# Reciprocals in four replicas, modulation rows next to the denominators, and another order of the down projection's pairs

## The chip, the cores and the metric

One core of one Trainium2 chip. The metric is the device time of one execution in microseconds (us). The program is written engine by engine: TensorE (PE in the profile; PEld are its weight loads), VectorE (DVE), ScalarE (ACT), GpSimd (POOL), and SyncE (SP), which issues nearly all DMAs.

## The reference, cut to what matters

A transformer block on x of 2048 rows by 1024 columns in bf16, with six modulation rows made from one vector c.

```python
mod = (silu(c) @ w_mod).reshape(1, 6, 1, -1)          # sa, ca, ga, sb, cb, gb
h = layernorm(x) * (1 + ca) + sa
x = x + ga * A(h)                                     # linear attention, 32 heads of 32
h = layernorm(x) * (1 + cb) + sb
x = x + gb * ((gelu(h @ w_gate) * (h @ w_up)) @ w_down)   # F = 3584

def A(h):
    q, k, v = heads(h @ wqkv)
    pq, pk = phi(q), phi(k)       # where(t > 0, t + 1, exp(t)) + 1e-6
    kv = einsum('bhsd,bhse->bhde', pk, v)
    z = einsum('bhsd->bhd', pk)
    num = einsum('bhqd,bhde->bhqe', pq, kv)
    den = einsum('bhqd,bhd->bhq', pq, z)[..., None] + 1e-6
    return merge(num / den) @ wo
```

## The kernel before, in words

Rows of x come in 16 chunks of 128, four to a group. The order of work on TensorE is the order in which the program calls its helpers; each helper hands operations to a scheduler object that finds the waits from the bytes that they touch. From the first k tiles to the end of the second FFN unit the orders of VectorE, ACT and GpSimd are rearranged by a small planner (`reorder`, with a table of costs); TensorE's and SP's orders stay as written, and in the down projection all orders are as written.

**Attention.** After keys and queries, 24 tiles `m_tile(g, k)` (L895) multiply phi(k) with the normalised rows, eight groups g of four heads, three column parts k; ACT copies each tile out (L900). When a group is whole, a DMA transpose (`m_t`, L703, tile mtb) turns it, and `kv_prod(g)` (L913) forms its kv blocks, which VectorE masks into KVT (L920). `w2_pair(i)` (L1201) multiplies kv blocks with wo rows into W2, 64x64 tiles of the array at a time; ACT or VectorE copies W2 out (L1208). `wo_mm` (L1283) then multiplies phi(q) with W2 and VectorE adds the result to x (L1291).

What happens between the tiles is listed in the table `HOOK` (L1302): tile number to a string of steps. `modp` and `gbr` are modulation rows: `mod_rows` (L840) sums partial products over partitions with eight matmuls onto 32 columns of the array each, ACT copies the row, and `mod_store` sends it to DRAM; two tiny loads (sbT, cbT, L1230) bring shift and scale back as columns. `den0` and `den1` are the denominators of half of the rows each: 32 matmuls onto 32 columns of the array (L1240), VectorE adds 1e-6 and takes the reciprocal (L1246) into RDC, 128 partitions (two groups, two halves, four heads of a group, eight groups g) by 256 rows, and `store` sends RDC to DRAM, scr_rd (L1248). `rb_load(sg, hs)` (L1260) brings the reciprocals back, each spread over the 32 partitions of its head: for each of the four heads of a group one DMA onto 32 partitions, 8 KB for each. `pq_scale` (L1273) multiplies phi(q) with them.

SP issues its DMAs in program order, and each waits until the DMA eight places before it has landed (eight lanes). All use one hardware queue.

**FFN.** 28 units (14 column pairs of w_gate and w_up, for each half of the rows). Each matrix product is done as one level of a 2x2 block scheme with seven products in place of eight (`prod`, numbers 1 to 7): products 1 and 2 take bf16 blocks as they are, 5, 6, 7, 3, 4 take sums of blocks in fp32r, made by VectorE (L1413, L1433). `wt_dma(u)` (L1371) loads a unit's weights. Results go to DRAM (scr_y).

**Down projection.** Eight pairs of chunks (`d_pair`), the same scheme: `d_prod(ca, b0, k)` (L1672) is 14 matmuls of 128x512 (weights are the activations' tile) of product k, operands `ya` (bf16, `y_in`, L1571), sums `sb` of ya blocks (`d_s`, L1648 on VectorE, L1643 on ACT) and sums `dt`, `dh` of w_down blocks (`d_t`, L1621), made once. A pair uses four of the eight PSUM banks, in turn with the next pair; `d_cp`, `d_ecp` (ACT) and `d_add` (VectorE) combine the products, and `evac` (L1576, L1577, then the output DMA L1578) multiplies with gb, adds x (`x_in`, L1568) and stores. `hook` calls of `hooks(i)` put DMAs and leftovers of pair 0 behind given products. Pair 0 has an order of its own (`d_pair0`), since its operands are only being made, and pair 1 still evacuates two parts of pair 0 and makes the last w_down sums.

The order of products in pairs 1 to 7, and the end of the list of steps:

```python
for k in (1, 5, 6, 2, 7, 3, 4):
...
elif k == 7:
    d_add(b0 + 3, b0 + 2)
    d_s(ca, 4)
    y_next(1)
    evac(*parts[3])
...
elif k == 3:
    evac(*parts[1])
    d_s(ca + 2, 0)
```

## Time and profile before

| What | Value |
|---|---|
| timed runs | 782.22, 783.16, 784.1 us (median 783.16) |
| profiled execution: first to last instruction | 780.9 us (780.946); it has no time of its own beside the span, and the median lies 2.2 us above it |
| granted TensorE clock | 1.000 |
| TensorE busy | 770.2 us, 99% of the span |
| VectorE busy | 645.9 us, 83% |
| ACT, GpSimd busy | 374.6 us (48%), 47.5 us (6%) |
| DMA | 130.22 MB, mean 167 GB/s; rb<-scr_rd 32 DMAs of 256 KB, 6.0 us from issue to landing |
| the tiles m, den, rows, W2 | 127.2 to 190.8 us |
| FFN units | 241.2 to 602 us (the last unit runs into the down projection) |
| down projection, pairs 1 to 7 | 623.5 to 777 us, 22.04 us for a pair |

A line of the order of time gives start, duration, engine, line, operation, output<-inputs, the shape and the count of instructions that were merged, and in brackets the idle time of the engine just before and what ended it. Weight loads are recorded at their own start, so the distance from one group's first load to the next group's is the time that the group holds TensorE.

### The profile page before, as it was taken

The page shows a single profiled execution, that of the slowest core. Times are in us where ns is not written, and L with a number is a line of the kernel's source. Part 1 is how long each engine was busy: PE and PEld are TensorE (multiplying, and loading weights), DVE is VectorE, ACT ScalarE, POOL GpSimd, SP SyncE. Part 2 cuts the span into 40 slices and gives each one's busy share as a digit, 9 for nine tenths or more (in the row PEclk, how much of TensorE's full clock was granted, in tenths as well). Part 3 has the DMA queues.
Part 4 walks back from the last instruction along what each step waited for, and adds up shares of the span by engine and source line. Part 5 has one row for each costly group of instructions (what it writes and reads, how often), then busy time and mean ns, then how long its engine had stood idle before and what let it go on. Part 6 is the DMA issues. An engine that isn't in the chain of part 4 may idle for free.

```text
span 780.9 us, 10753 instructions
## 1 busy us (share of the span) xinstructions
PE 770.2 (99%) x3825; PEld 496.2 (64%) x3883; DVE 645.9 (83%) x964; ACT 374.6 (48%) x629; POOL 47.5 (6%) x126
## 2 busy tenths in 40 slices
PE   8999999999999999999999999999999999999998
PEld 4444445666445667667676767667676576677766
DVE  6699988897899878787989888888989888676767
ACT  2497743242466487878755555555555211111111
POOL 2031300000321011100000000000000000000000
PEclk9999999999999999999999999999999999999999
DMA  9879749939999358867353865535356334443331
GB/s 284 256 167 252 158 91 215 255 80 196 203 287 231 82 138 212 230 175 215 99 145 108 250 211 172 148 96 161 97 147 221 111 127 139 144 141 114 126 125 60
DMA packets 196940, 130.22 MB, mean 167 GB/s; under 512 B 69516, under 2 KB 182420, under 8 KB 195864
## 3 DMA queue, kind: packets, MB, share of 16 engines
q1 hardware_dynamic: 196872, 129.55, 62.4%
q8 instruction: 30, 0.49, 0.3%
q14 instruction: 22, 0.18, 0.1%
q10 hardware_dynamic: 16, 0.00, 0.0%
HBM read 92.55 MB, written 23.35 MB: 148 GB/s over the span
## 4 chain that ended last, share of the span: by engine, by line
PE 95%; SPq 2%; DMA 1%; DVE 1%; issue 1%; ACT 0%; DVEq 0%; ACTq 0%
PE ps_all L1458 45%; PE ps_all L1672 21%; PE ps_all L895 7%; PE ps_all L934 7%; PE ps_all L1283 7%; PE ps_all L880 5%; PE ps_all L1593 1%; SPq L598 1%; DMA wmq<-in_w_mod_dram 1%; SPq L603 1%; DMA h1T<-xh 0%; PE ps_all L913 0%; PE ps_all L1201 0%; PE ps_all L1240 0%; DVE h1T L724 0%
## 5 line engine op out<-in xcount | busy, mean ns | idle before, releaser
L1458 PE MATMUL ps_all<-ss,tp 128*128 128x512 f32 x896 | 214.3, 396 | 0.0
L1458 PEld LDWEIGHTS ps_all<-ss,tp 128*128 128x128 f32 x896 | 168.3, 188 | 37.8 <-DVE ss L1413 0.2
L1672 PE MATMUL ps_all<-dt,sb 128*128 128x512 f32 x424 | 102.5, 398 | 0.0
L1481 ACT ACTIVATE ge<-ps_all 128x512 f32<-128x512 f32 x112 | 64.1, 597 | 73.8 <-DVE ps_all L1469 62.1
L1458 PE MATMUL ps_all<-h2a,wt 128*128 128x512 bf16 x421 | 95.7, 379 | 1.8
L1672 PEld LDWEIGHTS ps_all<-dt,sb 128*128 128x128 f32 x424 | 79.6, 188 | 18.5 <-DVE sb L1648 0.3
L1476 DVE TENSOR_TENSOR ps_all<-ps_all,es 128x512 f32<-128x512 f32 x54 | 37.6, 699 | 49.4 <-ACT es L1466 49.0
L1488 DVE TENSOR_TENSOR ys<-ge,ps_all 128x512 bf16<-128x512 f32 x112 | 74.4, 684 | 3.8 <-PE ps_all L1672 0.5
L1458 PEld LDWEIGHTS ps_all<-h2a,wt 128*128 128x128 bf16 x448 | 38.0, 98 | 57.3 <-ACT ps_all L1463 16.9
L1433 DVE TENSOR_TENSOR tp<-wt 128x1024 fp32r<-128x1024 bf16 x56 | 68.1, 1217 | 1.8 <-DMA wt<-in_B_w_up_dram 1.8
L1433 DVE TENSOR_TENSOR tp<-wt,tp 128x1024 fp32r<-128x1024 bf16 x56 | 68.2, 1218 | 0.0
L934 PE MATMUL ps_all<-h1T,wq 128*128 128x512 bf16 x256 | 56.7, 379 | 0.0
L880 PE MATMUL ps_all<-wk,h1T 128*128 128x512 bf16 x239 | 55.3, 379 | 1.1 <-DMA wk<-in_A_wqkv_dram 0.5
L1283 PE MATMUL ps_all<-w,pq 128*128 128x512 bf16 x249 | 55.7, 379 | 0.5 <-issue 0.2
L1458 PE MATMUL ps_all<-ar,tp 128*128 128x512 f32 x224 | 55.5, 390 | 0.0
L869 ACT ACTIVATE eb<-ps_all 128x512 f32<-128x512 f32 x64 | 36.3, 594 | 37.6 <-PE ps_all L880 16.0
L1672 PE MATMUL ps_all<-wd,ya 128*128 128x512 bf16 x199 | 47.5, 380 | 0.7
L1458 PEld LDWEIGHTS ps_all<-ar,tp 128*128 128x128 f32 x224 | 42.1, 188 | 8.9
L1463 ACT ACTIVATE ps_all<-ps_all 128x512 f32<-128x512 f32 x56 | 32.6, 582 | 26.8 <-PE ps_all L1458 26.5
L934 PEld LDWEIGHTS ps_all<-h1T,wq 128*128 128x128 bf16 x256 | 25.0, 98 | 30.0
L1283 PEld LDWEIGHTS ps_all<-w,pq 128*128 128x128 bf16 x256 | 24.6, 98 | 30.3 <-issue 1.1
L1643 ACT ACTIVATE sb<-ya 128x896 fp32r<-128x896 bf16 (+1 forms) x16 | 14.5, 913 | 58.8 <-PE ps_all L1672 58.8
(141 smaller groups left out, 976.3 us busy)
## 6 DMA issues: line engine op xcount, KB each, us to landing
wt<-in_B_w_gate_dram SPq DMA_DIRECT2D x28, 512.0 KB, 4.0
wt<-in_B_w_up_dram SPq DMA_DIRECT2D x28, 512.0 KB, 5.2
scr_y<-ys SPq DMA_DIRECT2D x28, 512.0 KB, 3.2
ya<-scr_y SPq DMA_DIRECT2D x14, 896.0 KB, 4.9
rb<-scr_rd SPq DMA_DIRECT2D x32, 256.0 KB, 6.0
wd<-in_B_w_down_dram SPq DMA_DIRECT2D x7, 1024.0 KB, 7.6
wmst<-in_w_mod_dram SPq DMA_DIRECT2D x6, 1024.0 KB, 6.2
wmq<-in_w_mod_dram SPq DMA_DIRECT2D x8, 512.0 KB, 7.5
```

What stands on the lines that cost most here:

```text
L869: sch.op(A, lambda e: e.activation(EB[i][:, :], PS(bank), ACTF.Exp), prd=pr(bank), wr=rng, note=f"{note}.exp")
L880: o = sch.op(T, lambda e, dc=dc: e.matmul(PS(bank), H1[sg][:, ci, dc, :], W_[:, dc, jg * 512:(jg + 1) * 512], start=(dc == 0), stop=(dc == ...
L895: o = sch.op(T, lambda e, c_=c_: e.matmul(PS(bank, 0, n), PK[c_][:, g * P:(g + 1) * P], xrow(c_, o_, o_ + n), start=(c_ == 0), stop=(c_ == ...
L934: o = sch.op(T, lambda e, dc=dc: e.matmul(PS(b), WQ[:, dc, qc * P:(qc + 1) * P], H1[sg][:, :, dc, :], start=(dc == 0), stop=(dc == NDC - 1 ...
L1283: last[half] = sch.op(T, lambda e, g=g, half=half: e.matmul(PS(b0 + half), PQ[sg][:, g, ci * P:(ci + 1) * P], W2[:, g, half * 512:(half + ...
L1433: sch.op(V, lambda e: e.tensor_tensor(TP[k][:], in0, in1 if k in (0, 2) else in1[:], ALU.subtract), rd=r0 + r1, wr=r_tp(k), deps=[x1_ops[7 ...
L1458: o = sch.op(T, lambda e, l_=l_, r_=r_, dc=dc: e.matmul(PS(b), l_, r_, start=fresh and dc == 0, stop=dc == ND2 - 1, skip_group_check=True) ...
L1463: sch.op(A, lambda e: e.activation(PS(BB + t), PS(BA + t), ACTF.Copy), prd=pr(BA + t), pwr=pr(BB + t), note="pcp")
L1476: sch.op(V, lambda e: e.tensor_tensor(PS(BC + t), PS(BC + t), ES[t][:, :], ALU.add), prd=pr(BC + t), rd=r_2k(OFF_ES[t], f"es{t}"), pwr=pr( ...
L1481: sch.op(A, lambda e: e.activation(GE[i][:, :], PS(b), ACTF.Gelu_apprx_tanh), prd=pr(b), wr=r_2k(OFF_GE[i], f"ge{i}"), note="gelu")
L1488: sch.op(V, lambda e: e.tensor_tensor(YS[s_][:, 2 * h:2 * h + 2, t, :], q(GE[i][:, :]), q(PS(b + 1)), ALU.mult), rd=r_2k(OFF_GE[i], f"ge{i ...
L1672: o = sch.op(T, lambda e, l_=l_, r_=r_, j=j, dst=dst: e.matmul(dst, l_[:, 0, :], r_, start=(k in (1, 5) or own is not None) and j == js[0] ...
```

## The change

1. The reciprocals are stored in four replicas (scr_rd has a dimension of four more; four DMAs from RDC, each to one replica), and `rb_load` brings them back with DMAs that span 128 partitions, two of the eight groups g at a time, 2 KB for each partition, with eight partitions reading one replica's row. `pq_scale` now waits for the part that it reads rather than for all loads of its half; two added dependencies keep VectorE's order (the first scale behind the second reciprocal, another behind the copy of W2 block 7).
2. The store of a denominator is a step of its own (`st0`, `st1`), behind the next transpose in SP's order.
3. `modp` goes from tile 15 to tile 16, directly ahead of `den0`, in bank 2 instead of 5; den0 uses bank 3; the second W2 pair (`w1`) directly follows den0. `gbr` directly follows `den1`, in bank 6. The loads of sbT and cbT become a step `sbl` at tile 22.
4. The first FFN unit's weights (`wt_dma(0)`) are issued right behind the reciprocals' loads instead of two chunks of wo later.
5. Pairs 1 to 6 of the down projection run products 5, 6, 7, 2, then product 1 of the next pair (`d_open`), 3, 4; product 1 of pair 1 comes ahead of the loop; pair 7 runs 5, 6, 2, 7, 3, 4. In pairs 1 to 6 product 7 starts a bank of its own (b0 + 3) and is joined by one more ACT copy and two adds (`d_join`) instead of one add. DMAs of x and the leftovers of pair 0 are moved to fit.

```diff
-    scr_rd = nc.dram_tensor("scr_rd", [NSG, 2, HPG, NG, SGW // 2], f32).ap()
+    NRP = 4
+    scr_rd = nc.dram_tensor("scr_rd", [NSG, 2, HPG, NRP, NG, SGW // 2], f32).ap()
...
         def mod_pass():
             assert mdone[0] >= 48 and not late
-            mod_rows(((2, 4, 5, hl_src),))
-            o_r = mod_store(4, 5, MROW[1], r_2k(OFF_ROW + 2048, "mrow1"), 1)
+            mod_rows(((2, 4, 2, hl_src),))
+            o_sc[0] = mod_store(4, 2, MROW[1], r_2k(OFF_ROW + 2048, "mrow1"), 1)
+
+        def mod_load():
             for dst, nt, a0 in ((SBT, "sbT", 0), (CBT, "cbT", 2)):
...
             def store():
-                o_rd[pr_] = sch.dma(Q, lambda e: e.dma_start(scr_rd[2 * pr_:2 * pr_ + 2].rearrange("s f k g t -> (s f k g) t"), RDC[:, :]),
-                          rd=r_sm("rdc"), note=f"rden{pr_}.st")
+                o_rd[pr_] = [sch.dma(Q, lambda e, r=r: e.dma_start(scr_rd[2 * pr_:2 * pr_ + 2, :, :, r, :, :].rearrange("s f k g t -> (s f k) g t"), RDC[:, :]),
+                                     rd=r_sm("rdc"), note=f"rden{pr_}.st") for r in range(NRP)]
...
         def rb_load(sg, hs=(0, 1)):
             i = sg % 2
             for h in hs:
-                for k in range(HPG):
-                    made.append(sch.dma(Q, lambda e, h=h, k=k: e.dma_start(
-                        RB[i][32 * k:32 * (k + 1), h, :, :].rearrange("p a b -> p (a b)"),
-                        scr_rd[sg, h, k:k + 1, :, :].rearrange("k g t -> k (g t)").to_broadcast([32, NG * HW])),
...
+                for g0 in range(0, NG, 2):
+                    src = scr_rd[sg, h, :, :, g0:g0 + 2, :].rearrange("k r g t -> (k r) (g t)").unsqueeze(1).to_broadcast([HPG * NRP, P // (HPG * NRP), 2 * HW])
+                    sch.dma(Q, lambda e, h=h, g0=g0, src=src: e.dma_start(
+                        RB[i][:, h, g0:g0 + 2, :].rearrange("p a b -> p (a b)"), src),
+                        wr=r_rb(i, h, g0, g0 + 2), deps=o_rd[sg // 2], note=f"rb{sg}.{h}.{g0}")
...
-        HOOK = {0: "ga", 6: "kv0", 10: "kv1", 11: "w0", 13: "kv2", 15: "modp kv3 z32", 16: "den0", 17: "w1 rb0.0 rb0.1", 18: "",
-                19: "kv4", 20: "den1 ps0.0", 21: "gbr", 22: "ps0.1", 23: "rb2.0"}
+        HOOK = {0: "ga", 6: "kv0", 10: "kv1", 11: "w0", 13: "kv2", 15: "kv3 z32", 16: "modp den0 w1", 17: "st0 rb0.0 rb0.1", 18: "",
+                19: "kv4", 20: "den1 gbr ps0.0", 22: "st1 sbl ps0.1", 23: "rb2.0"}
...
         rb_load(1)
         rb_load(2, (1,))
+        wt_dma(0)
...
-            b = b0 + {1: 0, 2: 0, 5: 3, 6: 2, 7: 2, 4: 2, 3: 1}[k] if own is None else own
+            b = b0 + {1: 0, 2: 0, 5: 3, 6: 2, 7: 3 if 0 < ca < 4 * CPG - 2 else 2, 4: 2, 3: 1}[k] if own is None else own
...
+        def d_join(b0):
+            d_ecp(b0 + 3)
+            d_add(b0 + 3, b0 + 1)
+            d_add(b0 + 2, b0 + 2)
+
+        def d_open(i):
+            b = i % 2 * 4
+            d_prod(2 * i, b, 1)
+            d_cp(b + 2, b, "dpcp")
...
-            for k in (1, 5, 6, 2, 7, 3, 4):
+            for k in ((5, 6, 2, 7, 3, 4) if last else (5, 6, 7, 2, 1, 3, 4)):
...
+                if k == 1:
+                    d_open(i + 1)
+                    hook(k)
+                    continue
                 d_prod(ca, b0, k)
-                if k == 1:
-                    d_cp(b0 + 2, b0, "dpcp")
...
+                elif k == 7:
+                    if last:
+                        d_add(b0 + 3, b0 + 2)
+                    else:
+                        d_join(b0)
+                    d_s(ca, 4)
+                    evac(*parts[3])
                 elif k == 2:
+                    y_next(1)
                     evac(*parts[0])
-                elif k == 7:
-                    d_add(b0 + 3, b0 + 2)
-                    d_s(ca, 4)
-                    y_next(1)
-                    evac(*parts[3])
...
-                4: lambda: (cb1(), wt_dma(0)),
+                4: lambda: cb1(),
...
-                    if k == 1:
-                        d_t(2, 5)
-                        d_t(2, 6)
-                    if k in (6, 2, 7):
-                        d_t(4, {6: 4, 2: 5, 7: 6}[k])
-                    if k in (6, 7):
+                    if k in (6, 2):
                         n = 1 if k == 6 else 2
                         evac(*parts_of(0)[n])
                         x_in(1, n)
+                    if k in (6, 7, 2):
+                        d_t(4, {6: 4, 7: 5, 2: 6}[k])
                 else:
-                    if k == 1:
-                        x_in(i, 0, 3, 1)
-                    elif k == 5:
-                        x_in(i, 2)
+                    if k == 5:
+                        x_in(i, 1, 2)
...
+                if more and k in (1, 4):
+                    x_in(i + 1, 3 if k == 1 else 0)
...
         d_pair0(hook0)
+        d_open(1)
+        d_t(2, 5)
+        d_t(2, 6)
```

## The prediction

> **What bounds the kernel now.** I read the page's busy times and its chain of waits first, then the order of time of TensorE's weight loads in the two places that are edited, then VectorE's and SyncE's order of time beside them.
>
> ```profile
> PE 770.2 (99%) x3825; PEld 496.2 (64%) x3883; DVE 645.9 (83%) x964; ACT 374.6 (48%) x629; POOL 47.5 (6%) x126
> ...
> PE 95%; SPq 2%; DMA 1%; DVE 1%; issue 1%; ACT 0%; DVEq 0%; ACTq 0%
> ```
>
> TensorE carries 95% of the chain that ends last. So only two things can move the end: TensorE's own stream getting shorter, or a new wait in it. Both edited stretches, 165 to 200 us and 598 to 777 us, already run without one wait for data (the listing of waits gives matmuls no releaser there), so no earlier load can pay by itself. What is left in TensorE's stream shows as idle time ahead of weight loads.
>
> ```profile
> 165.55 1.26 PEld L895 LDWEIGHTS ps_all<-xall,pk 128*128 128x128 bf16 x9
> 167.09 0.12 PEld L840 LDWEIGHTS ps_all<-hl,ones 128*32 128x32 bf16 x8 [0.28 <-issue]
> 167.63 0.45 PEld L913 LDWEIGHTS ps_all<-mtb,wv 128*128 128x128 bf16 x8 [0.42 <-issue]
> ...
> 183.88 1.26 PEld L895 LDWEIGHTS ps_all<-xall,pk 128*128 128x128 bf16 x9
> 185.42 0.12 PEld L840 LDWEIGHTS ps_all<-hlg,ones 128*32 128x32 bf16 x8 [0.28 <-issue]
> 185.75 0.84 PEld L895 LDWEIGHTS ps_all<-xrow,pk 128*128 128x128 bf16 x7 [0.21 <-issue]
> 186.64 1.26 PEld L895 LDWEIGHTS ps_all<-xall,pk 128*128 128x128 bf16 x9
> ```
>
> Nine loads of a plain tile that is followed by another take 1.30 us from their start to the next load; ahead of a stretch of narrow tiles they take 1.54 (183.88 to 185.42).
>
> ```profile
> 645.54 2.71 PEld L1672 LDWEIGHTS ps_all<-wd,ya 128*128 128x128 bf16 x14 [0.26 <-issue]
> 648.36 6.35 PEld L1672 LDWEIGHTS ps_all<-dt,sb 128*128 128x128 f32 x28
> 654.98 2.70 PEld L1672 LDWEIGHTS ps_all<-wd,ya 128*128 128x128 bf16 x14 [0.26 <-issue]
> 657.80 6.35 PEld L1672 LDWEIGHTS ps_all<-dt,sb 128*128 128x128 f32 x28
> 664.18 3.13 PEld L1672 LDWEIGHTS ps_all<-dh,sb 128*128 128x128 f32 x14
> 667.58 2.71 PEld L1672 LDWEIGHTS ps_all<-wd,ya 128*128 128x128 bf16 x14 [0.26 <-issue]
> ```
>
> This is one pair of the down projection, 22.04 us, and the next one repeats it to the hundredth.
>
> **The change part by part.**
>
> *Rows beside the denominators.* Three stretches of narrow tiles lose their own place among the 128-wide tiles: the eight matmuls of the modulation rows go directly ahead of den0, the first units of W2 (pair 1) directly behind den0, the gb rows directly behind den1. What a stretch costs beyond its columns: with the gb rows, 183.88 to 186.64 is 2.76 us; without them 1.30 + 1.02 = 2.32; so 0.44 for two rounds of 256 columns, which take 0.108 each inside den's own stretch: 0.22. The modulation rows: 1.54 + 0.54 + 0.41 - 1.30 - 0.54 = 0.65, less two rounds of 512 columns at 0.216: 0.22. The W2 units (172.38 to 175.37): 2.99 - 2.32 = 0.67, less 2 x 0.23: 0.21. The rows have den's tile shape (128x32), so I take their 0.22 twice, less two hundredths each: 0.20 + 0.20. The W2 units are 64x64; the trace has no step from 128x32 to 64x64. Bounds: 0.21 saved, if the step is free, or nothing, if it costs as much as leaving for 128-wide tiles and coming back; I take the middle, 0.10. Sum 0.50, between 0.40 and 0.61.
> By the Trainium skill, TensorEngine Tiling (Array Packing), Key Properties, a change of the tiling mode, though not of the tile, drains TensorE. The idle loads above bear that out; by it the W2 stretch keeps one of its two drains, and the sum would be 0.50 as well, where a count by stretches alone gives 0.61.
>
> *Down pairs in another order.* Before, a pair runs bf16, 28 fp32r, bf16, 28 + 14 fp32r; afterwards (pairs 1 to 6) 5, 6, 7, 2, then product 1 of the next pair, 3, 4: one bf16 stretch in place of two. From the lines above, 14 fp32r matmuls in the middle of a run take 3.17 us (the stretch of 42 from 657.80, 9.78, less the one of 28 from 648.36, 6.61 before rounding); so 28 of them are 6.35 and the stretch shows 6.61: 0.26 for entering and leaving. A bf16 stretch of 14 is 2.82 where 14 x 0.216 is 3.02: 0.20 back. A switch pair costs 0.06 to 0.07 net. Fourteen changes into fp32r become eight: 6 x 0.065 = 0.39 saved. The matmuls are the same in number and kind.
>
> *What it adds.* Each pair 1 to 6 gains an ACT copy (L1698, 0.60) and a VectorE add (L1695, 0.70), since product 7 has a bank of its own. ACT has 7 to 8 us free per pair; VectorE is busy 14.9 of 22.04 us in a pair from the third on, so there both hide. But product 5 now follows product 4 directly, and its first operand (L1648, the sums of the next pair) is made after product 3: product 3's last load, 0.42 to VectorE's start (686.23 to 686.65 in the trace), two evacuation steps 1.41, half a sum 1.09 = 2.92 of the 3.17 that product 4 lasts. Margin 0.25, so nothing in the steady pairs. In pair 1 VectorE has more to do:
>
> ```profile
> 640.82 0.69 DVE L1695 TENSOR_TENSOR ps_all<-ps_all,de 128x512 f32<-128x512 f32 x1
> 641.54 0.70 DVE L1576 TENSOR_TENSOR ps_all<-ps_all,gbb 128x512 f32<-128x512 f32 x1
> ...
> 645.49 0.69 DVE L1576 TENSOR_TENSOR ps_all<-ps_all,gbb 128x512 f32<-128x512 f32 x1
> 646.28 0.69 DVE L1577 TENSOR_TENSOR xq<-ps_all,xq 128x512 bf16<-128x512 f32 x1
> 647.06 2.09 DVE L1648 TENSOR_TENSOR sb<-ya,ya 128x896 fp32r<-128x896 bf16 x2
> ```
>
> It runs without a gap from 633.8 to 652.5, with four leftovers of pair 0 and three weight sums (L1621, 1.21 each). The first half of the sums ends at 647.06 + 1.09 = 648.15, and TensorE takes it at 648.36: 0.21 to spare. The new add is one more step of 0.62 to 0.79 ahead of it on the same engine, while product 5 is due at the same moment as before, since product 1 only moved ahead of 3 and 4. So the half ends at 648.8 to 648.9, and TensorE waits 0.45 to 0.7, once: I take 0.55. Behind the late sums stand the sums for product 6 (due 3.17 later, made 2.1 later) and the evacuation of part 2; both catch up.
>
> *The reciprocals.* Instead of one store (128 KB) and eight loads onto 32 partitions each, there are four stores and eight loads onto 128. SP issues six DMAs more, and now sends: row store, transpose mT4 (waits for ACT's copy of tile 17, about 175.1), four stores, eight loads, mT5, gb row store, mT6, four stores, sbT, cbT, mT7, then as before. Who waits: kv5 for mT5, kv6 and kv7 for mT6 and mT7.
>
> ```profile
> 176.69 3.76 SPq L1260 DMA_DIRECT2D rb<-scr_rd  x8
> 180.55 1.23 SPq L703 DMA_TRANSPOSE mtb<-mb  x1
> ```
>
> Transfers land in the order of issue. Before: first load lands at 180.26, the eighth at 188.62 (1.16 to 1.2 apart), mT5 at 189.58, kv5 begins at 190.28. Afterwards: mT4 issued by 176.4, four stores at 0.35 to 0.81 to about 178, the last landing 2.24 after its issue, 180.2; first load 3.2 later, 183.4. A 2,048-byte packet onto 128 partitions takes 84 to 89 ns, an 8,192-byte packet of the old loads 605, so a load needs 8 x 0.087 = 0.70 instead of 1.16: the eighth lands at 188.3, mT5 0.96 later, 189.3, and kv5 comes at 190.28 - 0.48 = 189.80. Hidden, with 0.5 to spare; with 1.16 it would be 192.5. mT7 is issued at 190.5 (when ACT has copied tile 23), lands 3.07 later if nothing is in its way, 193.6, up to 194.6 behind sbT and cbT (3.9 each from issue); kv7 comes at 194.5. I take 0.1 for both places. sbT and cbT, moved by 17 us, are first read at 213.1 (L1767).
>
> *The first unit's weights*, moved ahead of the h2 transposes, and the second reciprocals only gain: VectorE's 1.45 us wait at 199.83 and its 1.8 us wait for wt at 224.04 should go. No matmul waits for either, so they are worth nothing at the end. The transposes come no later: SP has issued the two loads by about 204, and ACT ends the first transpose's rows at 209.8.
>
> **Sum.** -0.50 - 0.39 + 0.55 + 0.1 = -0.24 us on the profiled span of 780.95: 780.7. The timed median 783.16 lies 2.2 above that span, so 782.9.
>
> **Rivals.** (B) No new wait at all: -0.50 - 0.39, 782.2 (782.0 with the larger tile saving). For it: every margin above is positive except the one in pair 1; against it: that one is short by a whole add. (C) Slower: mT5 is late. If the loads keep 1.16, mT5 lands at 192.5 and kv5 waits 2.7, mT7 another 0.5 to 1: -0.89 + 0.55 + 3.4 = +3.1, 786.2; it decides from 0.77 per load on, and half-way (stores landing 1 us later) the time is 783.9 to 784.5. For it: the loads start 3.7 later than before; against it: the packets of other loads. By the Trainium skill, SBUF — State Buffer, The DMA setup-cost knee, every transfer pays about 2 us whatever its size; four stores paid one after another would be an estimated 8 us and kv5 over 4 us late, 787; the trace speaks against it, since old loads issued 0.45 apart land 1.16 apart. (D) Slower: the margin of 0.25 fails in all later pairs, 5 x 0.3 to 0.6 = 1.5 to 3: 784.4 to 786. For it: VectorE has a step more and the operand half the slack; against: 14.9 of 22 us busy.
>
> **How the numbers follow.** Forecast 0.48 (782.3 to 783.7), B 0.22, C 0.14, D 0.10, another gain 0.06. A difference of 0.2% is 1.57 us, about what a measurement of this kernel can tell from no change; the three runs shown spread by 1.9. Faster by more needs twice the savings found: 0.07 with a part of B's tail. Slower by more: most of C and D, 0.22. The rest, 0.71, within. Range: from below B, 781.8, to the middle of C and D, 785.2.
>
> **What would show it.** In the changed profile: no narrow stretch at 167 or 185, den's stretches 0.5 us longer; TensorE pairs of 21.97 us; one wait for VectorE (L1648's sums) of about half a microsecond at pair 2's product 5; loads 0.7 apart; mT5 landed before kv5. Wrong if kv5 or kv7 names a DMA, or if the wait at product 5 comes back in each pair.

## The result

The changed kernel takes 786.85 us (median of 5, 786.26 to 787.23) where the kernel before takes 782.59 on the same chip: 1.0050 times, 95% interval 1.0038 to 1.0062. It is slower by 4.3 us; the forecast was 782.9. The profiled execution took 786.26, its span is 784.46 us, 3.51 more than the span before (780.95).

Where it went, from the first weight loads of the same steps in both traces:

| stretch, us | before | after | difference |
|---|---|---|---|
| start to den1's first load | 182.00 | 181.39 | -0.61 (0.29 of it is there at 160 us already, before any changed step) |
| den1 to the FFN's first load | 59.24 | 63.74 | +4.50 |
| FFN to down's first dh product | 380.21 | 380.13 | -0.09 |
| down's first dh product to the end | 159.49 | 159.20 | -0.29 |

So the parts that were meant to save TensorE time do save, and the attention's last 60 us lose more. In the page of the changed kernel, TensorE's busy time hardly differs (770.2 before). In the chain that ended last DMA has 2% instead of 1%:

```profile
PE 771.2 (98%) x3829; PEld 497.2 (63%) x3883; DVE 647.7 (83%) x970; ACT 376.7 (48%) x635; POOL 48.2 (6%) x126
...
PE 95%; SPq 2%; DMA 2%; issue 1%; DVE 1%; DVEq 0%
```

Read in the order of time, this chain has a piece that was not there before (start, duration), the transpose mT5:

```profile
185.51 7.01 DMA mtb<-mb
```

The list of TensorE's waits names it (total, number, longest):

```profile
PE ps_all L914 <- DMA mtb<-mb: 2.8, 1, 2.8
```

That is kv5, waiting for the transpose mT5. TensorE's order of time around it, after:

```profile
188.27 1.47 PE L896 MATMUL ps_all<-xall,pk 128*128 128x342 bf16 x9
192.57 0.62 PE L914 MATMUL ps_all<-mtb,wv 128*128 128x128 bf16 x8 [2.83 <-DMA mtb<-mb]
193.25 3.19 PE L1288 MATMUL ps_all<-w,pq 128*128 128x512 bf16 x7
196.36 0.74 PE L1204 MATMUL ps_all<-wo,kvt 64*64 64x512 bf16 x8
```

The nine weight loads ahead of kv5 hold TensorE for 4.44 us; elsewhere nine such loads hold it for 1.31: +3.13. But the row below is odd as well. The seven matmuls of 512 columns start 427 ns apart, twice their usual 216: the granted clock fell (columns: window, its length, busy time of PE, PEld, DVE, ACT, POOL, clock, share of the DMA engines, GB/s).

```profile
189.50:192.50 3.00, 0.24 (x2) 0.00 (x0) 2.08 (x3) 0.46 (x1) 0.00 (x0) 1.00 1.16 159
193.20:196.60 3.40, 3.35 (x11) 1.06 (x14) 0.45 (x2) 0.00 (x0) 0.00 (x0) 0.51 0.74 138
```

And this is what SP sent in that time, after (start, duration of the issuing):

```profile
174.62 1.26 SPq L704 DMA_TRANSPOSE mtb<-mb  x1
175.93 2.51 SPq L1255 DMA_DIRECT2D scr_rd<-rdc  x4
180.35 5.06 SPq L1267 DMA_DIRECT2D rb<-scr_rd  x8
185.51 1.36 SPq L704 DMA_TRANSPOSE mtb<-mb  x1
186.98 0.54 SPq L850 DMA_DIRECT2D scr_row<-mrg  x1
187.62 3.86 SPq L704 DMA_TRANSPOSE mtb<-mb  x1
191.57 2.49 SPq L1255 DMA_DIRECT2D scr_rd<-rdc  x4
194.10 0.59 SPq L1237 DMA_DIRECT2D sbT<-scr_row  x1
194.75 0.68 SPq L1237 DMA_DIRECT2D cbT<-scr_row  x1
195.54 1.33 SPq L704 DMA_TRANSPOSE mtb<-mb  x1
```

The four transposes are mT4 to mT7. mT5 leaves at 185.51 (180.55 before) and lands at 192.53 (189.58 before); mT7 leaves at 195.54 (191.15 before) and lands at 198.78 (194.22 before). Where the issuing is long, SP is held up.

From kv7's first weight load to the FFN's it is 46.25 us, 46.27 before. So all that the attention loses, it has lost when kv7 begins.

### The profile page after: what moved, and what is told of

It is laid out like the page before. It is cut to its first block, busy times and chain, and to the rows that moved or that the text cites. A ratio compares the mean times of both kernels' runs of the same rounds, so it can differ in the third digit from the quotient of the medians.

```text
span 784.5 us, 10775 instructions
## 1 busy us (share of the span) xinstructions
PE 771.2 (98%) x3829; PEld 497.2 (63%) x3883; DVE 647.7 (83%) x970; ACT 376.7 (48%) x635; POOL 48.2 (6%) x126
## 4 chain that ended last, share of the span: by engine, by line
PE 95%; SPq 2%; DMA 2%; issue 1%; DVE 1%; DVEq 0%
PE ps_all L1467 45%; PE ps_all L1681 21%; PE ps_all L1288 7%; PE ps_all L935 7%; PE ps_all L896 6%; PE ps_all L881 6%; PE ps_all L1602 1%; SPq L599 1%; DMA wmq<-in_w_mod_dram 1%; DMA mtb<-mb 1%; SPq L604 1%; PE ps_all L914 0%; PE ps_all L1204 0%; PE ps_all L1247 0%; SPq L593 0%
## 5 line engine op out<-in xcount | busy, mean ns | idle before, releaser
L1467 PE MATMUL ps_all<-ss,tp 128*128 128x512 f32 x896 | 214.3, 396 | 0.0
L1467 PEld LDWEIGHTS ps_all<-ss,tp 128*128 128x128 f32 x896 | 168.4, 188 | 37.7 <-DVE ss L1422 0.2
L1467 PE MATMUL ps_all<-h2a,wt 128*128 128x512 bf16 x421 | 95.6, 379 | 1.8
L1467 PEld LDWEIGHTS ps_all<-h2a,wt 128*128 128x128 bf16 x448 | 37.9, 97 | 57.3 <-ACT ps_all L1472 16.9
L1288 PE MATMUL ps_all<-w,pq 128*128 128x512 bf16 x249 | 57.2, 387 | 0.5 <-issue 0.2
L1467 PE MATMUL ps_all<-ar,tp 128*128 128x512 f32 x224 | 55.5, 390 | 0.0
L1707 ACT ACTIVATE de<-ps_all 128x512 f32<-128x512 f32 x14 | 8.4, 597 | 90.2 <-PE ps_all L1681 90.2
L1467 PEld LDWEIGHTS ps_all<-ar,tp 128*128 128x128 f32 x224 | 42.1, 188 | 8.8
L1681 PE MATMUL ps_all<-wd,ya 128*128 128x512 bf16 x203 | 45.9, 380 | 0.6
L1288 PEld LDWEIGHTS ps_all<-w,pq 128*128 128x128 bf16 x256 | 24.9, 99 | 31.1 <-issue 2.6
```

The lines of the kernel that those rows point to most:

```text
L1288: last[half] = sch.op(T, lambda e, g=g, half=half: e.matmul(PS(b0 + half), PQ[sg][:, g, ci * P:(ci + 1) * P], W2[:, g, half * 512:(half + ...
L1467: o = sch.op(T, lambda e, l_=l_, r_=r_, dc=dc: e.matmul(PS(b), l_, r_, start=fresh and dc == 0, stop=dc == ND2 - 1, skip_group_check=True) ...
L1681: o = sch.op(T, lambda e, l_=l_, r_=r_, j=j, dst=dst: e.matmul(dst, l_[:, 0, :], r_, start=(k in (1, 5) or k == 7 and 0 < ca < 4 * CPG - 2 ...
```

## The experiments

One table for all, so that the runs can be compared: medians, the ratio to the kernel before measured beside it with its 95% interval, and four lengths from the profiled execution. "kv5" and "kv7" are counted from den1's first weight load to kv5's first load and kv7's first matmul, "FFN" from den1 to the FFN's first load, "units" from there to down's first dh product. Where one run alone was made, a difference of 1 us in its time says little.

| kernel | time | ratio | kv5 | kv7 | FFN | units |
|---|---|---|---|---|---|---|
| before | 782.6 to 783.2 | 1 | 8.28 | 13.02 | 59.24 | 380.21 |
| changed | 786.85 | 1.0038 to 1.0062 | 11.18 | 17.52 | 63.74 | 380.13 |
| rb0.1 behind mT5 | 787.61 | 1.0043 to 1.0069 | 8.05 | 16.78 | 64.40 | 380.13 |
| half of rb0.1 behind mT5 | 785.70 | 1.0027 to 1.0054 | 9.41 | 16.32 | 62.54 | 380.13 |
| one store, wide loads | 834.91 | 1.0645 to 1.0673 | 21.84 | 28.29 | 101.85 | 389.73 |
| one store, old loads, changed place | 786.35 | 1.0029 to 1.0053 | 10.30 | 14.91 | 61.55 | 381.62 |
| all transposes first | 786.68 | 1.0031 to 1.0055 | 8.28 | 13.46 | 61.52 | 381.68 |
| old reciprocals, old place | 784.27 | 1.0005 to 1.0022 | 8.28 | 13.02 | 59.99 | 381.69 |
| before + down order | 782.84 | 0.9989 to 1.0006 | 8.28 | 13.01 | 59.23 | 380.16 |
| eight replicas | 793.71 | one run | 13.44 | 22.34 | 70.14 | 380.16 |
| before + early weights | 785.13 | 1.0015 to 1.0038 | 8.28 | 13.02 | 60.02 | 381.68 |
| old reciprocals, late weights | 782.63 | 0.9988 to 1.0006 | 8.28 | 13.02 | 59.66 | 380.13 |
| changed, late weights | 786.36 | 1.0028 to 1.0054 | 10.86 | 17.16 | 63.38 | 380.15 |
| all transposes first, late weights | 784.42 | 1.0012 to 1.0030 | 8.28 | 13.68 | 60.91 | 380.53 |
| changed, late weights, wait filled | 786.69 | 1.0034 to 1.0061 | 11.06 | 17.23 | 63.45 | 380.12 |
| 128 rows read | 785.03 | one run | 10.32 | 15.82 | 62.04 | 380.11 |
| four loads of 512 KB | 789.74 | one run | 12.30 | 18.29 | 64.70 | 381.61 |

### Is it mT5, and what puts it late?

**rb0.1 behind mT5.** The first theory was that mT5's place behind eight loads is the whole cause.

```diff
-  17: "st0 rb0.0 rb0.1", ..., 19: "kv4"
+  17: "st0 rb0.0", ..., 19: "kv4 rb0.1"
```

> The changed kernel with one step moved: SP issues the four reciprocal loads of the second half (rb0.1) behind the transpose mT5 instead of ahead of it. Theory (SP's order): in the changed kernel mT5 stood behind four stores and eight loads that came 1.07 us apart, landed at 192.53 and held TensorE 3.13 us at kv5 (9 loads took 4.439 instead of 1.306); the clock's fall to 0.5 and wo's first eight matmuls at 3.384 instead of 1.873 come from that wait. Then mT5 is issued at about 182.9, lands at 187 to 188.5, ahead of 189.4 when kv5 is due: no wait at kv5, no row with a clock of 0.5 near 193, wo's first eight at 1.87, the FFN's first load at 240.3 to 240.7 instead of 245.13; span 779.7 to 780.3, time 781.6 to 782.6. Rival 1 (the transpose itself is slow among other traffic: 7.0 us from issue to landing wherever it is put): lands at 189.9, kv5 waits 0.5, 782.7. Rival 2 (the halved clock is not the wait's): wo's first eight keep 3.4, 783.6.

mT5 landed at 188.50 and kv5 waited for nothing, as expected, and the time did not fall at all. TensorE's order of time in this kernel:

```profile
189.80 0.61 PE L914 MATMUL ps_all<-mtb,wv 128*128 128x128 bf16 x8
...
194.58 0.62 PE L914 MATMUL ps_all<-mtb,wv 128*128 128x128 bf16 x8 [0.49 <-DMA mtb<-mb]
198.38 1.01 PE L914 MATMUL ps_all<-mtb,wv 128*128 128x128 bf16 x8 [3.18 <-DMA mtb<-mb]
199.18 1.91 PE L1288 MATMUL ps_all<-w,pq 128*128 128x512 bf16 x4
```

kv7 now waits 3.18 us for mT7, and the clock falls behind that wait (four wo matmuls in 1.91 us). SP sent mT7 at 194.12, behind four stores that took 3.23 to issue, sbT and cbT:

```profile
189.34 3.23 SPq L1255 DMA_DIRECT2D scr_rd<-rdc  x4
192.95 0.40 SPq L1237 DMA_DIRECT2D sbT<-scr_row  x1
193.62 0.39 SPq L1237 DMA_DIRECT2D cbT<-scr_row  x1
194.12 2.21 SPq L704 DMA_TRANSPOSE mtb<-mb  x1
```

The first theory falls in its second half: mT5 is not the cause that decides. In the changed kernel the wait at kv5 had covered a second one at kv7. That the FFN starts 0.7 later here than in the changed kernel, although kv7 comes 0.7 earlier, is the half clock, which now lies behind the last wait, where nothing covers it: from kv7's first load to the FFN's 47.66 us instead of 46.25.

**Half of rb0.1 behind mT5.**

```diff
-  17: "st0 rb0.0 rb0.1", ..., 19: "kv4"
+  17: "st0 rb0.0 <first two loads of rb0.1>", ..., 19: "kv4 <last two>"
```

> The changed kernel with two of the four loads of rb0.1 ahead of mT5 and two behind it. Theory (SP's order): the sixth load lands at about 189.7 as in the changed kernel, mT5 0.9 later at 190.5, kv5 waits 1.0 to 1.2 instead of 3.13. If the clock falls only after a wait near 3 us, wo's first eight stay at 1.87 and the time is 782.9 to 783.3; if any wait halves it, another 1.5: 784.5.

mT5 landed at 190.70 and kv5 waited 1.1 (expected 1.0 to 1.2), with the clock at 1.0; but 785.70, not 783, because kv7 waited another 2.1: the same second wait.

**One store, wide loads.**

```diff
-    NRP = 4
+    NRP = 1
```

> The changed kernel with one replica: one store instead of four, the loads still over 128 partitions. Theory (SP's order, the four stores cost 1.9 us ahead of the loads): the store is issued at 175.9 and lands at 178.2, the first load is issued at 178.3 instead of 180.35, the eighth lands at 189.7, mT5 at 190.6, kv5 waits 1.1; 783.0 to 783.5 if the clock does not fall. Rival (the four rows in DRAM are what the wide loads are fast by): with one row read by 32 partitions the loads come 1.2 or more apart, mT5 lands at 191.5 or later and kv5 waits 2 or more, 784 to 785.5.

50 us slower, which neither side expected. Stretches of this kernel and of the changed one (columns as above):

```profile
184.00:188.00 4.00, 4.00 (x29) 2.68 (x28) 2.91 (x3) 0.53 (x2) 0.00 (x0) 1.00 0.28 107
```

```profile
184.00:188.00 4.00, 4.00 (x30) 2.65 (x29) 3.67 (x5) 0.91 (x2) 0.00 (x0) 1.00 1.01 271
```

The DMA engines are busy for 28% instead of 101%. Of the wide loads' packets 4.2 are in flight on average between 184 and 202 us, and they take 84 ns each; 101% in the changed kernel's stretch is 16 packets in flight. So a load whose source has four rows runs on four DMA engines, and the four replicas in DRAM (16 rows) are what puts a wide load on all sixteen. They cannot be dropped one by one.

**One store, old loads, in the changed kernel's place.**

```diff
-    NRP = 4
+    NRP = 1
-    rb_load: eight loads onto 128 partitions
+    rb_load: eight loads onto 32 partitions, as before
```

> The changed kernel with the store and the loads of the kernel before (one store, each load 256 KB onto 32 partitions), both in the changed kernel's place, that is behind mT4. Theory: the store lands at 178.2, the first load at 181.9, 1.17 apart, the eighth at 190.1, mT5 at 191.0; kv5 waits 1.6 to 1.9; 783.6 to 784.2, or 1.5 more if the clock falls. Against the run with one store and wide loads this gives the price of the loads' width (0.7 over eight loads), against the changed kernel that of the four stores. Rival (width is worth what the prediction said, 0.46 per load): the two differ by 3.7.

The loads landed 1.2 apart from 181.05 on, the eighth at 189.47, mT5 at 191.67; kv5 waited 1.9. mT7, with three stores less ahead of it, was in time. It left at 192.43, when kv5 had ended (192.34): it fills the buffer that kv5 reads, so each delay of kv5 is passed on to it, which the prediction's condition (ACT's copy) does not name. kv5 came 0.88 earlier than in the changed kernel: there replicas and wide loads together cost time instead of saving it. Still 786.35 instead of 783.6 to 784.2: the FFN starts 2.3 later than before, counted from den1, and the units take 381.62 instead of 380.13. There is a third wait, further down.

### The third wait

**All transposes first.** Both groups that SP has ahead of a transpose moved behind it.

```diff
-  17: "st0 rb0.0 rb0.1", 19: "kv4", ..., 22: "st1 sbl ps0.1", 23: "rb2.0"
+  17: "st0 rb0.0", 19: "kv4 rb0.1", ..., 22: "ps0.1", 23: "st1 sbl rb2.0"
```

> The changed kernel with all three transposes ahead of what the change added to SP's order: rb0.1's four loads behind mT5, and the second four stores with sbT and cbT behind mT7. In the run with only rb0.1 moved, kv5 waited for nothing, but mT7 was issued at 194.12 and kv7 waited 3.2. Theory (it is SP's order: whatever stands behind the added stores and loads is late, first mT5, then mT7): mT5 lands at about 188.5, mT7 is issued at 190.3 to 190.6 and lands at 193.5 to 194.6, where kv7 is due at 195.0; no wait at either, no half clock, the first wo load to the FFN's first 50.0 to 50.6 instead of 55.8 there and 52.2 in the changed kernel; span 779.8 to 780.6, time 781.7 to 782.7. Rival (the transposes are slow because the reciprocal loads fill the DMA engines, wherever they stand): mT7 lands at 195.5 or later, kv7 waits 1 or more, 783 and above.

Both waits for transposes are gone but for 0.3, no half clock in any of five executions, and 786.68. TensorE's waits in this kernel:

```profile
PE ps_all L1467 <- DVE xall L1296: 1.0, 2, 0.5
PE ps_all L1288 <- DVE pq L1278: 0.8, 1, 0.8
...
PE ps_all L1467 <- DVE ss L1422: 0.5, 2, 0.3
PE ps_all L914 <- DMA mtb<-mb: 0.3, 1, 0.3
```

VectorE is late at the FFN's start (L1467) and once in wo (L1288).

**Old reciprocals in the old place**, all else as changed.

```diff
-    NRP = 4, four stores behind mT4, wide loads
+    one store ahead of mT4, loads onto 32 partitions
```

> The changed kernel with only the reciprocals undone: one store right behind den, ahead of mT4, and the old eight loads onto 32 partitions, in the order of the kernel before; the modulation rows, W2's units and the gb rows stay beside den0 and den1, and so do the down pairs' order and the early weights. Theory: the rest of the change gains 0.55 in the tiles and 0.28 in down; kv5 comes 0.55 earlier than before, so that mT5 is just in time (a wait of 0.3 at most). From den1's first load to kv5's 8.05 to 8.35 (8.275 before, 11.18 in the changed kernel); time 0.5 to 0.9 below the kernel before. Rival (the moved rows or the early weights cost something themselves): level with the kernel before or above it.

kv5 and kv7 wait for nothing and the tiles' saving is there (below), but 784.27, slower than before: the rival, "the early weights cost something themselves". VectorE stood still for 4.38 us at 218.9 until the h2 transposes had landed, then ran without a gap to 255; wo to the FFN cost 0.75 more, the units 1.5.

This kernel and the one with the old loads in the changed place differ only in where the stores stand. With the first store behind mT4, mT5 landed at 191.67 and kv5 came at 10.30; with it ahead, at 188.89 and 8.28. So with the old loads, part 2 of the change costs 2.0 us at kv5 and about 2 us of the time (786.35 against 784.27); the prediction took it to be hidden.

**The early weights alone**, on the kernel before.

```diff
         rb_load(2, (1,))
+        wt_dma(0)
...
-                 4: lambda: (cb1(), wt_dma(0)),
+                 4: lambda: cb1(),
```

> The kernel before with only the first unit's two weight loads moved up in SP's order, behind rb2.1 and ahead of the h2 transposes, as in the changed kernel. Theory: the first h2 transpose, which stood ahead of the weights and landed at 215.97, now stands behind them and lands at about 219, the second at 223; VectorE waits about 4 us for them at 219 (no wait there before), runs without a gap to 255 and is late with the FFN's sums: TensorE waits 0.3 to 1.0 on VectorE at the FFN's start and 1.5 in its first 15 us. From the FFN's first load to down's first dh 381.6 to 381.8 instead of 380.21; 784.4 to 785.2. The prediction's value for this part (nothing at the end) gives no difference.

785.13, as expected. VectorE before, and with this edit (L724 scales the transposed h2):

```profile
217.65 1.22 DVE L1291 SCALAR_TENSOR_TENSOR xall<-ps_all,xall 128x1024 bf16<-128x1024 f32 x1
...
218.90 2.14 DVE L724 TENSOR_SCALAR h2a<-h2a,cb1T,sbT 128x256 bf16<-128x256 bf16 x8
```

```profile
217.92 1.22 DVE L1291 SCALAR_TENSOR_TENSOR xall<-ps_all,xall 128x1024 bf16<-128x1024 f32 x1
...
223.98 2.14 DVE L724 TENSOR_SCALAR h2a<-h2a,cb1T,sbT 128x256 bf16<-128x256 bf16 x8 [4.84 <-issue]
```

The first h2 transpose in SP's order, before and with this edit:

```profile
209.87 1.23 SPq L703 DMA_TRANSPOSE h2a<-xl  x1
```

```profile
210.20 7.25 SPq L703 DMA_TRANSPOSE h2a<-xl  x1
```

It took 7.25 us to issue behind the two weight loads (1.23 before); the issuing ended at 217.45, just ahead of the landing of the first of them (217.53). It landed at 219.96 instead of 215.97, the next at 223.90 instead of 218.82. VectorE's wait for the weights themselves (1.8 us before) is gone, and a wait of 4.84 has taken its place.

**Changed, weights late again**, and **old reciprocals, weights late again**, and **all transposes first, weights late again** (the edit above, reversed).

> The changed kernel with only the first unit's weights back behind the h2 transposes. Theory: there the FFN starts 3.9 us later than before for kv5's wait, which hides VectorE's wait for the transposes (2.38 at 225.08); taking the early weights away gains nothing: 786.3 to 787.2, FFN to dh 380.1 as in the changed kernel. Rival (early weights cost 2 wherever they are): 784.8.

> The changed kernel without its two DMA parts: reciprocals by one store and eight loads as before, and the first unit's weights back behind the h2 transposes; the rows beside the denominators and the order of the down pairs stay. Theory: in the run with the reciprocals undone and the early weights kept, TensorE lost 0.75 between wo's first load and the FFN's and 1.5 in the FFN, to VectorE and so to the late h2 transposes; both go. From den1's to kv5's first load 8.28, wo to FFN 50.4, FFN to down's first dh 380.1 to 380.2; 0.3 to 0.7 below the kernel before, 782.2 to 782.6. Rival (the moved rows delay VectorE themselves): 784 as in that run.

> The kernel with all transposes mT5 to mT7 ahead of the added transfers, and in addition the first unit's weights behind the h2 transposes, as before. Theory: with the mT order alone, kv5 and kv7 waited 0.3 together, but TensorE lost 1.85 between kv7 and the FFN (1.0 for the scaling of the second half, behind late reciprocal loads; 0.85 at the FFN's start) and 1.5 in the FFN. The 0.85 and the 1.5 are those of the late h2 transposes and go; the 1.0 stays: 783.4 to 784.2. If the wide loads behind the transposes delay h2 as much as the weights did, 785 or more.

786.36: in the changed kernel the late h2 transposes are covered by the later FFN start, as expected. 782.63: without the two DMA parts the units are back at 380.13 and the time is level with the kernel before: what the rest of the change gains is too small to be measured, and 0.4 of it goes to a wait for VectorE's scaling (L1277) at 206.5, so wo to the FFN took 50.85 and not the expected 50.4. 784.42: this is 2.3 less than with the transposes first and the weights early; what is left is a wait of TensorE that ends at 208.1 and costs 1.0 us, for the scaling L1278 behind late loads, and kv7, 0.66 later than before.

### The half clock

**The wait filled.** On the changed kernel with late weights, 16 matmuls into an unused bank ahead of kv5.

```diff
             if n == len(tiles) - 1:
+                for i in range(16): matmul(PS(7, 0, 342), PK[0][:, 0:P], xrow(0, 0, 342))
                 kv_prod(5, 4)
```

> The changed kernel with the first unit's weights behind the h2 transposes, and 16 more matmuls of 342 columns (2.3 us, into a free PSUM bank, their result unused) ahead of kv5, so that TensorE works through the stretch in which it waited for mT5. Without them kv5 began at 192.72, the clock fell to 0.5 for 3.4 us, wo's first eight matmuls took 2.94 instead of 1.87, and the span was 784.55. Theory (the clock falls for TensorE's idle time): kv5 begins when it did, within 0.2; no row of the clock below 1.0 there; wo's first load to the FFN's 50.4 instead of 52.1; the median falls by 0.8 to 1.7 from 786.36, to 784.7 to 785.6. Rival (the halved clock costs nothing at the end, since something else sets the FFN's start): wo to FFN 52, 786.0 to 786.6.

The clock stayed at 0.999 or above in all five executions and wo's first eight matmuls took 1.87 us (3.50 without the filling; the 2.94 of the expectation was misread). Still it took 786.69, the rival's time, and 51.98 from wo to the FFN. TensorE's order of time:

```profile
190.87 2.48 PE L1341 MATMUL ps_all<-xrow,pk 128*128 128x342 bf16 x16
193.51 0.62 PE L914 MATMUL ps_all<-mtb,wv 128*128 128x128 bf16 x8 [0.16 <-DMA mtb<-mb]
...
197.68 0.61 PE L914 MATMUL ps_all<-mtb,wv 128*128 128x128 bf16 x8
199.68 0.61 PE L914 MATMUL ps_all<-mtb,wv 128*128 128x128 bf16 x8 [1.40 <-DMA mtb<-mb]
```

What the full clock saves is waited at kv7. That is the answer to what decides in the changed kernel: mT7. There mT7 landed at 198.78 and kv7's first matmul started 0.13 later, as in the runs in which it plainly waits (0.13 to 0.14); without the transpose it would have started at 198.82, 0.055 behind the matmul before it. So TensorE reached kv7 0.1 us too early, with the wait at kv5 and the half clock both used up on the way. In the changed kernel neither of the two is a price of its own.

### What a wide load costs

**Eight replicas**, **128 rows**, **four loads of 512 KB**.

```diff
-    NRP = 4
+    NRP = 8
```

> The changed kernel with eight replicas instead of four: eight stores, and each wide load reads 32 rows in DRAM, four partitions each, instead of 16 rows by eight. For the price of the wide loads: a packet of 2,048 bytes took 84 in the median and 117 ns in the mean there, and 1.07 us a load; with one replica only 4 packets were in flight instead of 16. If what slows the packets is that eight partitions read the same row, the mean falls to 85 to 100 and the loads come 0.75 to 0.85 apart. If it is something on the receiving side, it stays at 110 to 130. Four more stores delay mT5 by 2.5: kv5 waits 4 to 6, 788 to 790.

```diff
-    src = scr_rd[sg, h, :, :, g0:g0 + 2, :] ... .to_broadcast([16, 8, 2 * HW])
+    src = scr_rd[sg].rearrange("h k r (a g) t -> (h k r a) (g t)", g=2)
```

> The changed kernel, where each wide reciprocal load reads 128 different rows of the stored block, one per partition, instead of 16 rows by eight partitions; what it loads is not what belongs to the partition, so the scaled values are wrong, and only the times count. Bytes, packets, destination and order stay. If the reading of the same row slowed the loads (117 ns per packet, 1.07 us per load), they now come 0.70 to 0.80 apart at 85 to 95 ns, mT5 lands at 190 and kv5 waits 0.6. If it is the receiving side or the engines' other work, they stay at 1.0 to 1.1 and kv5 waits about 3.

```diff
-    for g0 in range(0, NG, 2):     # 2,048-byte rows
+    for g0 in range(0, NG, 4):     # 4,096-byte rows
```

> The changed kernel with four wide loads of 512 KB (rows of 4,096 bytes) instead of eight of 256 KB for each two stretches of chunks. If the price is by the byte, the loads come 2.1 apart and mT5 lands at 192.5 as before the edit; if a part of the 1.07 belongs to each load, they come 1.4 to 1.8 apart and mT5 lands at 189.5 to 191.5.

In the changed kernel the first of the eight landed at 184.18, the eighth at 191.66: 1.07 apart. With eight replicas it was 186.31 to 193.76, 1.06 apart: no gain, against the expectation. kv5 waited 4.9 and kv7 another 2.8, 793.71 instead of 788 to 790. With 128 different rows it was 183.36 to 189.51, 0.88 apart; of the steps seen singly four were 0.64 to 0.68 and one 1.39. But mT5 landed 2.5 after the last of them, at 191.98, so kv5 still waited: from the first load's landing to mT5's it was 8.6, against 8.2 to 8.4 in the three traces with the shared rows (changed, and with late weights without and with the filling). Issuing such a load took SP 0.43, the shared one 0.60. Rows of 4,096 bytes, shared by eight, took 266 ns a packet, and the loads landed 2.2, 2.2 and 3.5 apart: more than twice the 1.07, so nothing is gained by fewer loads.

The mean of the packets does not decide it either: 117 ns in the changed kernel's trace, but 105 and 106 in the two others with the same loads, 107 with eight replicas and 104 with 128 rows. And with shared rows the last three steps were 0.65 to 0.81 behind one of 2.1 (late weights), and 0.53 to 0.77 behind one of 2.6 (late weights, wait filled). So these traces, one for each kernel, show no price of the repeated rows that is clear of their spread. What they show is loads that come 0.5 to 0.8 apart and now and then stop; why they stop is open.

### The order of the down pairs alone

**Down alone**, on the kernel before: the hunks of the diff that concern `d_prod`, `d_join`, `d_open`, `d_pair` and their hooks.

> The kernel before with only the new order of the down pairs. Theory: six pairs of switches less at 0.065 and one wait of under 0.2 at pair 2's product 5: from the first load of the first pair's own operands (621.45) to those of the last (773.03) 151.25 to 151.35 instead of 151.57; the whole time 0.2 to 0.35 below the kernel before, under what its executions differ by. The prediction's sizes (0.39 saved, 0.55 lost) would make it 0.16 slower.

782.84 against 783.00, no difference that can be measured. From the first dh product to the last one's 151.51 instead of 151.57, less than expected in this trace: its first pair lost 0.3 in its bf16 stretch (6.15 us for 28 loads, 5.84 in the next pairs). In the changed kernel the same distance is 151.29.

## Why the prediction was wrong

**The step that failed** is that of the reciprocals: "a load needs 8 x 0.087 = 0.70 instead of 1.16", and behind it "I take 0.1 for both places". The four stores landed when the sum said (180.21; 180.2 predicted), the first load 0.8 later than it said (184.18; 183.4), and then the loads came 1.07 apart. mT5 landed 3.2 later than predicted (192.53; 189.3) and kv5 waited 2.8. The 84 to 89 ns were what a packet takes in other transfers. The median here is 85, too, but the mean is 117, and single steps of over 1 us (1.6 the longest seen singly in this trace) stand between those of 0.7 to 0.9: the sum had no term for loads that stop. For both places together it took 0.1; kv7 came 4.50 later than before, 4.7 with the 0.23 that the gb rows had saved by then.

**The term that was missing** is larger in its effect: "mT7 is issued at 190.5 (when ACT has copied tile 23)". SP was not free then. mT6's issuing took 3.86 us, four stores 2.49, sbT and cbT 1.4 with their gaps, so mT7 left at 195.54. The late loads are a part of this, since mT6's issuing ended only at 191.48, 0.2 ahead of the eighth load's landing. With the loads as predicted (the eighth at 188.3) the same steps would give about 192 for mT7, an estimate, and so a wait at kv7 still. The runs with mT5 moved and with the wait filled show that this, not mT5, set the time: whichever of the two waits is taken away, the other has its place, and the time stays between 785.7 and 787.6; with both gone the h2 transposes keep it at 786.7.

**The early weights**, "worth nothing at the end", cost time by themselves: 785.13 against 782.87 alone on the kernel before (1.0015 to 1.0038), and 1.6 between the two kernels with old reciprocals. "The transposes come no later" counted SP's time for issuing the weights (0.4 each) and not that the next transpose then took 7.25 us to issue. In the changed kernel this is hidden by the late FFN start (786.36 with the weights late again, 786.85 without).

**Rival C** described the course: loads at 1.16, mT5 at 192.5, a wait of 2.7, mT7 behind it, 786.2. Its condition, "from 0.77 per load on", was met. For mT7 it had 0.5 to 1; measured are 1.6 (kv7 4.50 late, kv5 2.90), most of it spent at the half clock, which it did not have. That its total comes within 0.7 is in part luck. It had a chance of 0.14 because the packets of other loads were given more weight than the loads onto the same tile, which the trace showed 1.16 apart.

By the Trainium skill, SBUF — State Buffer, The DMA setup-cost knee, every transfer pays about 2 us; taken as four stores that pay it one after another, the trace disagrees: they landed 0.55 to 0.76 apart. The estimate of 787 built on it was near by luck.

**Rows beside the denominators**: predicted 0.50 saved, measured 0.55. From the tile ahead of it all to den1's first load 21.22 instead of 21.54 (0.33 for the modulation rows and W2's units), and den1 to kv5 8.05 instead of 8.28 (0.23 for the gb rows; read in the run with rb0.1 behind mT5, since kv5 waits in the changed kernel). In both of these traces the gb rows take 0.43 to the next tile. In seven of the kernels above (old reciprocals in the old place and all transposes first among them) they took 0.65, and the second part was not there: only 0.33 was left. What makes the difference is open. In the kernel without the two DMA parts the wait for the scaling took the 0.33 away.

**Down's order**: pairs of 21.97 as predicted (9.74 + 5.85 + 3.21 + 3.17). The weight loads of the second pair:

```profile
648.97 3.13 PEld L1681 LDWEIGHTS ps_all<-dh,sb 128*128 128x128 f32 x14
652.30 9.39 PEld L1681 LDWEIGHTS ps_all<-dt,sb 128*128 128x128 f32 x42 [0.20 <-DVE sb L1657]
661.95 5.73 PEld L1681 LDWEIGHTS ps_all<-wd,ya 128*128 128x128 bf16 x28 [0.26 <-issue]
667.80 3.17 PEld L1681 LDWEIGHTS ps_all<-dt,sb 128*128 128x128 f32 x14
```

**The wait at product 5 of pair 2**, predicted at 0.55, is 0.16 (3.33 instead of 3.17 for the 14 loads ahead of it). The place was right; the size was not. The sums' first half ended 24.92 us after pair 1 began, 24.62 before: VectorE's busy time in this stretch grew by 0.42 only (22.34 instead of 21.92), since two adds in a row take 1.29 together, and 0.12 of its idle time was used up. Sum of down: -0.29 instead of +0.16.

## What to carry to other kernels

A queue that is issued in order is a stage of its own: when transfers are put into it, follow every later consumer on it with the time at which the queue itself is free, not only the one next behind, and look for waits that hide one another, since here kv5, kv7 and the FFN's start each covered the next, and undoing one alone gained little. A wait can also be passed on: mT7 fills the buffer that kv5 reads. Price a transfer by the distance between landings of such transfers, not by its median packet alone, which has no term for pauses. A prefetch that is moved up pays only if what it passes in the queue has slack.

## What the runs showed of the hardware

**The clock after an idle stretch.** Behind TensorE's idle 2.83 us at kv5 the granted clock was 0.5 for 3.413 us, from 193.24 to 196.66 in the changed kernel's trace, and 0.5 for the same 3.413 us behind 3.18 us at kv7 in the run with rb0.1 moved. It fell so after 2.51 us, too (changed, late weights), and not in the profiled executions with 2.13 us (half of rb0.1, at kv7) and 1.95 us (one store, old loads). With the gap filled by matmuls it did not fall. Where the limit lies was not measured; three of the changed kernel's five executions fell, two did not, and those two were no shorter (spans 785.2 and 785.4 against 784.5 to 785.1). The stretches of the clock's record are whole multiples of 3.413 us in the longest disturbance, too: 13.653, 17.067 and 6.827 in the run with one store and wide loads.
The Trainium skill, TensorE: Matmul & The Clock Gate, What's actually happening, has the clock halved after an idle window of about 3.4 us that runs freely, 3,413 ns long; the length agrees, and here an idle stretch a little shorter than a window was enough.

**DMA engines by source rows.** Four source rows gave 4.2 packets of the wide loads in flight; with sixteen the DMA engines had 16 packets in flight (101% of 16 engines at 184 to 188 us). The Trainium skill, DMA: Bandwidth & Descriptors, Rules for kernel authors, says that a leading dimension of fewer than 16 confines a transfer to at most that many engines; the trace agrees.

**A transpose's issuing is held by transfers ahead of it.** Transposes that take about 1.25 us to issue otherwise took 3.86 (mT6, changed), 3.45 (mT6, old loads), 2.93 (mT6, 128 rows) and 7.25 us (h2, early weights alone). In each of these the issuing ended 0.05 to 0.35 us ahead of the landing of a transfer two or three places before it in the queue: 191.48 and 191.66, 189.12 and 189.47, 189.46 and 189.51 (the eighth load each time), 217.45 and 217.53 (the first weight load). It is not the transpose before that holds it: mT5 landed 1.05, 2.5 and 2.5 us after the end of mT6's issuing, and in the last case the transpose before had landed at 194.54 already. What the queue runs out of is not shown, and no run was made for it alone.
